# Decode attention with a gated MLP on one core: the up projection in 12 small pieces instead of 3 bursts

## The chip, the core and the metric

The kernel runs on one core of a Trainium2 chip. The core has five engines with instruction queues of their own: TensorE (PE in the profile; PEld is its weight load), VectorE (DVE), ScalarE (ACT), GpSimd (POOL) and SyncE (SP), which here only issues transfers. Each queue runs in order; engines wait for one another through semaphores. 16 DMA engines move data between the device memory and the on-chip buffer. The metric is the device time of one execution in microseconds (us); lower is better.

## The reference, cut to what matters

One decode step for a batch of B = 8, D = 576, 32 heads of 128, 4096 cached keys and values per head, and beside it an MLP with a hidden width of 4608; a gate mixes the two.

```python
q = (x @ wq).reshape(B, 1, 32, 128).transpose(0, 2, 1, 3)
scores = einsum("bhqd,bhkd->bhqk", q, k_cache) * 128 ** -0.5
o = einsum("bhqk,bhkd->bhqd", softmax(scores), v_cache)
a = o.transpose(0, 2, 1, 3).reshape(B, 1, 4096) @ wo
...
h = gelu(einsum("bsd,df->bsf", layernorm(x), w1) + b1)
b = einsum("bsf,fd->bsd", h, w2) + b2
...
g = sigmoid((x * gate_w).sum(-1, keepdims=True))
out = g * a + (1 - g) * b
```

The K and V caches are 256 MiB each in bf16 and are read once. The weights come to about 20 MB.

## The kernel before, in words

**Groups.** The (batch, head) pairs are worked in 32 groups of 8 heads of one batch (`NG` = 32, loop at L593). A group has 8 MiB of K and 8 MiB of V: the 128 partitions are 8 heads x 16 stretches of the sequence, each with 256 positions. K comes in two halves of 128 positions (4 MiB each) into two buffers `KB0` and `KB1`; V comes whole into one buffer, `VB`.

**Scores.** A half has four chunks of 32 positions, so a group has eight, c = 0 to 7. For a chunk DVE multiplies K by q into `p1`, which has two halves used in turn (`mult`, L413); TensorE sums pieces of the 128 products with eight matmuls against a resident identity (`p_sum`, L424 for the first, L169 for the seven others, which keep the stationary operand); DVE reduces the result into `s_sb` (`reduce`, L431). `scores` (L435) writes the order out by hand: mult 0, mult 1, then for every c: reduce c, mult c + 2. After each mult, with its eight matmuls, it calls `between(c)`, which places other work at that point of the queues. `mult(c + 2)` waits for the matmuls of chunk c, and the matmuls of a chunk wait for the reduce two chunks back.

**Softmax, P·V and after.** `softmax` (L447) makes the maximum, the exponentials (ACT, L457), the probabilities `P` (L460) and their sum on DVE. On TensorE follow `total` (L481) and 64 matmuls of P against `VB` (`pv`, L474), then ACT's eviction (L486) and `gather` (L491). `norm` of group n - 1 runs on DVE behind mult 1 of group n.

**The queue of transfers.** All large loads go out on SP in program order: x, wq, K and V of group 0, w1 (two parts, L393, waiting for the q projection, since wq, w1, w2 and wo use one buffer, `RB`), and then in every group n the two K halves of n + 1 and V of n + 1. A half of K waits until `mult` 3 or 7 has read the buffer (`k_done`); V waits until `pv(n)` has read `VB` (`v_done`). An issue that waits on SP holds up what is behind it.

**The MLP around the change.** `up_proj(j0, j1)` (L504) runs 6 matmuls with 8 moving columns each for every one of the 36 tiles of the hidden width (`NJ`): 4 with a 128-wide and 2 with a 64-wide stationary operand, into the PSUM bank `up_ps`; 216 in all. Before the change it runs in 3 calls of 12 tiles (72 matmuls), behind chunk 6 of group 1 and chunks 2 and 6 of group 2. `act_h` (L515) is the gelu: five DVE operations and a sigmoid on ACT, behind chunk 7 of group 2. `load_w2` and `load_b2` follow at the end of group 2. `down_proj` (L547, `quarters` at L533) runs 36 x 4 matmuls in two calls of 18 tiles in group 4, `b_out` (L552) behind them; `load_wo` follows at the end of group 4. `a_proj` uses wo from group 30 on. TensorE's instructions are written out for groups 0 to 4 and from 29 on; groups 5 to 28 are one loop of 24 turns (`emit_loop`, L97; `L0`, `L1`).

Of the kernel before, what the change touches and what calls it, by code (L numbers as in the profile page):

```python
# [20 lines left out]
NJ = F // 128  # L21
# [3 lines left out]
NHG = H // HB  # L25
NG = NHG * B
NTT = SK // RH
NKH = 2
NTK = NTT // NKH
CT = 32  # L30
NCK = NTK // CT
NC = NKH * NCK
# [9 lines left out]
class Stream:  # L42
# [9 lines left out]
    def op(self, engine, fn, waits=(), dma=None):  # L52

        rec = [fn, [w for w in waits if w is not None], None, dma]
        self.ops[engine].append(rec)
        if dma is not None:
            return ("dma", *dma)
        return ("op", engine, rec)
# [75 lines left out]
def bass_gated_mix__mha_block_cached__mixer_channel_mlp__decode_kernel(  # L134
# [20 lines left out]
    def pstride(t):  # L155
        return t[tuple([slice(None)] * len(t.shape))].ap[0][0]
# [122 lines left out]
    def load_k(u):  # L279
        n, s = divmod(u, NKH)  # L280
        nK[s] += 1
        src = kv_src(A_k_cache, n)[:, s * NTK:(s + 1) * NTK, :]
        k_land[u] = op("sync", lambda e: e.dma_start(KB[s][:, :, :], src), [k_done.get(u - NKH)], dma=(sK[s], 16 * nK[s]))
# [7 lines left out]
    def load_v_part(n, buf, at, t0, t1, waits):  # L291

        src = kv_src(A_v_cache, n)[:, t0:t1, :]
        dst = buf[:, at:at + t1 - t0, :]
        t = load("sync", dst, src, f"sVp{n}_{t0}", waits)
        v_land.setdefault(n, []).append((t, buf, at - t0, t0, t1))
# [102 lines left out]
    def q_of(b):  # L399
        for i in range(2):  # L400
            t = op("tensor", lambda e, i=i: e.matmul(
                qb_ps[64 * i:64 * i + 64, :], lhsT=Sel[:, b, :],
                rhs=bass.AP(tensor=Q4, offset=i * DH, ap=[[pstride(Q4), 128], [2 * DH, NHG], [1, DH]]),
                start=True, stop=True), [*a_Q, c_Sel, a_qb.get(b - 1)] if i == 0 else ())
        a_qb[b] = op("scalar", lambda e: e.activation(out=q_bc[:, b, :], in_=qb_ps[:, :], func=ACT.Copy), [t])
# [29 lines left out]
    def scores(n, between):  # L435

        mult(n, 0)
        between(0)
        mult(n, 1)
        between(1)  # L440
        for c in range(NC):
            reduce(n, c)
            if c + 2 < NC:
                mult(n, c + 2)
                between(c + 2)
# [34 lines left out]
    def total(n):  # L480
        p_z[n] = op("tensor", lambda e: e.matmul(  # L481
            oz_ps[:, HB:2 * HB], lhsT=ones[:, :], rhs=rs[:, :], start=True, stop=True),
            [v_rs[n], v_norm.get(n - 1), c_ones])
# [11 lines left out]
    def norm(n):  # L495
        hg, b = divmod(n, B)
        t = op("vector", lambda e: e.reciprocal(out=rz[:, :], in_=oz_ps[:, HB:2 * HB]), [p_oz[n]])  # L497
        v_norm[n] = op("vector", lambda e: e.tensor_tensor(
            out=OT_sb[:, hg * HB:(hg + 1) * HB, b], in0=oz_ps[:, 0:HB], in1=rz[:, :], op=ALU.mult), [t])
# [4 lines left out]
    def up_proj(j0, j1):  # L504
        for jt in range(j0, j1):
            for kt in range(NKF + 2):
                o, n, at = up_ps[:, jt * B:(jt + 1) * B], 128, kt * F + jt
                if kt >= NKF:
                    o, n, at = up_ps[64 * (kt - NKF):64 * (kt - NKF) + 64, jt * B:(jt + 1) * B], 64, NKF * F + jt
                w = bass.AP(tensor=RB, offset=at, ap=[[pstride(RB), 128], [NJ, n]])  # L510
                st["p_up"] = op("tensor", lambda e, w=w, o=o, kt=kt: e.matmul(  # L511
                    o, lhsT=w, rhs=yT_sb[:, kt, :], start=(kt == 0), stop=(kt >= NKF)),
                    [*ld_w1, v_yT] if jt == kt == 0 else ())

    def act_h():  # L515
        hb, t2 = (up[:, i, :] for i in range(2))
        b1b = bass.AP(tensor=b1_sb, offset=0, ap=[[pstride(b1_sb), 128], [1, NJ], [0, B]])
        t = op("vector", lambda e: e.tensor_tensor(
            out=hb.rearrange("p (f b) -> p f b", b=B), in0=up_ps[:, 0:NJ * B].rearrange("p (f b) -> p f b", b=B),
            in1=b1b, op=ALU.add), [st["p_up"], ld_b1])  # L520
        st["v_hb"] = t
        t = op("vector", lambda e: e.tensor_tensor(out=t2, in0=hb, in1=hb, op=ALU.mult), [t])
        t = op("vector", lambda e: e.tensor_scalar(out=t2, in0=t2, scalar1=0.044715, scalar2=1.0, op0=ALU.mult,
                                                   op1=ALU.add), [t])
        t = op("vector", lambda e: e.tensor_tensor(out=t2, in0=t2, in1=hb, op=ALU.mult), [t])
        t = op("scalar", lambda e: e.activation(out=t2, in_=t2, func=ACT.Sigmoid, scale=gelu_c), [t])
        st["v_h"] = op("vector", lambda e: e.tensor_tensor(
            out=hT_sb[:].rearrange("p f b -> p (f b)"), in0=hb, in1=t2, op=ALU.mult), [t])
# [4 lines left out]
    def quarters(lhsT, w, first, stop, waits):  # L533

        for i in range(4):
            last = op("tensor", lambda e, i=i: e.matmul(
                y_ps[32 * i:32 * i + B, 0:QN], lhsT=lhsT, rhs=w[:, i * QN:(i + 1) * QN], start=first, stop=stop),
                waits if i == 0 else ())
        return last
# [7 lines left out]
    def down_proj(j0, j1):  # L547
        for jt in range(j0, j1):
            st["p_down"] = quarters(hT_sb[:, jt, :], w2_sb[:, jt, :], jt == 0, jt == NJ - 1,
                                    [st["ld_w2"], st["v_h"], c_yps] if jt == 0 else ())  # L550

    def b_out():  # L552
        st["v_bx"] = op("vector", lambda e: e.tensor_tensor(
            out=bmg_sb[0:QP, :], in0=y_ps[0:QP, 0:QN], in1=b2_4[0:QP, :], op=ALU.add), [st["p_down"], *st["ld_b2"]])
        st["v_bmg"] = op("vector", lambda e: e.tensor_scalar(
            out=bmg_sb[0:QP, :], in0=bmg_sb[0:QP, :], scalar1=g4[0:QP, 1:2], scalar2=None, op0=ALU.mult),
            [st["v_bx"], v_g4])
# [4 lines left out]
    def a_proj(hg):  # L562
        for h in range(hg * HB, (hg + 1) * HB):
            st["p_a"] = quarters(OT_sb[:, h, :], wo_sb[:, h, :], h == 0, h == H - 1,
                                 [v_norm[hg * B + B - 1], st["ld_wo"], st["v_bx"]] if h == hg * HB else ())
# [17 lines left out]
            [p_oz[n], v_rz[n]])  # L583


    UP0, UPN = 3, 3
    DN = 4
    AP = 30
    L0, L1 = 5, 29
    done_a = [0]  # L590
    last = NG - 1
    q_of(0)
    for n in range(NG):  # L593
        if L0 <= n <= L1:
            S.marks.append(len(S.ops["tensor"]))

        def between(c, n=n):
            u = n * NKH + c // NCK
            c4 = c % NCK
            if c == 1 and 1 <= n < last:  # L600
                norm(n - 1)
            if n == last and c == NCK:
                load_v_part(n, KB[0], 0, 0, NTK, [k_done[NKH * n]])
                t0 = NTK
                for nt in V_LAST:
                    load_v_part(n, VB, t0 - NTK, t0, t0 + nt, [p_pv[n - 1]])
                    t0 += nt
            if c4 == 2:
                if UP0 <= u < UP0 + UPN:
                    up_proj((u - UP0) * NJ // UPN, (u - UP0 + 1) * NJ // UPN)  # L610
                if n == DN:
                    down_proj((c // NCK) * NJ // 2, (c // NCK + 1) * NJ // 2)
                if n >= AP and done_a[0] < NHG - 1:
                    a_proj(done_a[0])
                    done_a[0] += 1
            if c4 == 3:
                if u == UP0 + UPN - 1:
                    act_h()
                if n == DN and c > NCK:
                    b_out()  # L620
            if n == 0 and c + 1 < B:
                q_of(c + 1)

        scores(n, between)
        softmax(n)
        if n < last:
            total(n)
        if n < last - 1:
            load_k(NKH * (n + 1))
            load_k(NKH * (n + 1) + 1)  # L630
            pv(n, (0,))
            evict(n)
            gather(n)
            if n + 1 < last - 1:
                load_v(n + 1)
        if n == last - 2:
            load_v_part(last - 1, VB, 0, 0, NTK, [v_done[n]])
        if n == last - 1:
            load_k(NKH * last)
            load_k(NKH * last + 1)  # L640
            load_v_part(n, VB, NTK, NTK, NTT, [v_done[n - 1]])
            pv(n, (0,))
        if n * NKH <= UP0 + UPN - 1 <= n * NKH + 1:
            load_w2()
            load_b2()
        if n == DN:
            load_wo()
# [60 lines left out]
```

## Time and profile before

| | us |
|---|---|
| median of 3 runs | 1315.97 (1313.71 to 1316.01) |
| the profiled execution | 1315.18 |
| its span, first to last instruction | 1313.4 |
| TensorE busy in it | 815.9 (62%) |
| VectorE busy | 856.8 (65%) |
| ScalarE busy | 47.9 (4%) |
| read from memory | 556.96 MB, 424 GB/s over the span |

How to read the profile: times are from the start of the span. The page divides the span into 40 slices of 32.8 us and gives a busy share of each in tenths, the clock that TensorE was granted (PEclk; 1.0 is full speed), and the DMA engines' busy share. Groups of instructions are named by line, engine, operation and tiles (out<-in), with count, busy time, mean length of one in ns, and the idle time of the engine ahead of them with what ended it (`<-`). "The chain" is the work that ended last, followed back step by step to what released it. Rows of the timeline give start, length, engine, line, operation and tile names; equal neighbours are merged (x72 is 72 instructions), and a matmul's end is modelled, so neighbouring rows can overlap a little.

### The profile page before, as it was taken

To read this page: it belongs to the slowest core of one execution; us is meant where nothing else is said; L and a number is where in the kernel's file an instruction comes from. 1 tells how busy PE (TensorE), PEld (TensorE's weight loads), DVE (VectorE), ACT (ScalarE), POOL (GpSimd) and SP (SyncE) were. 2 spreads that over 40 slices of the span, in tenths; PEclk is the share of its full clock that TensorE was granted. 3 is DMA by queue.
4 is the path that set the end of the run, shared out by engine and by line. 5 is a ranking of instruction groups with operands and counts; after the bars stand their busy time and mean duration, and the time that the engine had idled before them with its cause. 6 is when DMAs were issued, how large, how long until landed. Compare 5 with 4: busy or idle time off the path is not lost.

```text
span 1313.4 us, 10207 instructions
## 1 busy us (share of the span) xinstructions
PE 815.9 (62%) x5156; PEld 170.7 (13%) x3364; DVE 856.8 (65%) x1094; ACT 47.9 (4%) x81; POOL 1.6 (0%) x12
## 2 busy tenths in 40 slices
PE   3647765655666666666565666565666666666666
PEld 0103311110111100111110111110111110011113
DVE  4565574556666677666677666668665667766685
ACT  1100000000000000000000000000000000000000
POOL 0000000000000000000000000000000000000000
PEclk8867797887887888787888878888977888878788
DMA  9999989999999999999999999999999999999997
GB/s 400 426 437 442 392 357 442 432 408 446 423 441 418 432 431 432 442 431 439 420 431 434 443 425 439 420 433 433 433 444 423 439 422 431 433 444 428 425 403 292
DMA packets 20904, 557.28 MB, mean 424 GB/s; under 512 B 2048, under 2 KB 6160, under 8 KB 7056
## 3 DMA queue, kind: packets, MB, share of 16 engines
q1 hardware_dynamic: 20624, 556.95, 98.7%
q8 instruction: 13, 0.21, 0.1%
q14 instruction: 11, 0.09, 0.0%
q10 hardware_dynamic: 256, 0.03, 0.0%
HBM read 556.96 MB, written 0.01 MB: 424 GB/s over the span
## 4 chain that ended last, share of the span: by engine, by line
DMA 64%; DVE 21%; PE 13%; issue 0%; SPq 0%; ACT 0%
DMA KB<-in_A_k_cache_dram 63%; DVE p L413 17%; PE psb L169 8%; DVE s_sb L431 4%; DMA VB<-in_A_v_cache_dram 2%; PE psb L424 2%; PE psb L511 1%; PE psb L474 1%; SPq L250 0%; DVE P L460 0%; PE psb L491 0%; PE psb L481 0%; ACT E L457 0%; DVE mA L448 0%; ACT O_sb L486 0%
## 5 line engine op out<-in xcount | busy, mean ns | idle before, releaser
L413 DVE TENSOR_TENSOR p<-KB,q_bc 128x4096 bf16<-128x4096 bf16 x256 | 581.9, 2283 | 310.3 <-DMA KB<-in_A_k_cache_dram 310.3
L169 PE MATMUL psb<-p,ident 128*128 128x512 bf16 x1792 | 487.8, 418 | 0.0
L424 PE MATMUL psb<-p,ident 128*128 128x512 bf16 x256 | 111.6, 436 | 299.2 <-DVE p L413 298.8
L431 DVE TENSOR_REDUCE s_sb<-psb 128x32 f32<-128x512 f32 x256 | 175.6, 686 | 91.8 <-PE psb L169 91.6
L474 PE MATMUL psb<-VB,P 128*32 128x512 bf16 x1984 | 176.5, 534 | 0.3 <-DMA VB<-in_A_v_cache_dram 0.2
L424 PEld LDWEIGHTS psb<-p,ident 128*128 128x128 bf16 x256 | 26.4, 103 | 738.9 <-DVE p L413 651.2
L481 PE MATMUL psb<-rs,ones 128*128 128x8 f32 x64 | 18.8, 367 | 155.5 <-DVE rs L464 154.9
L474 PEld LDWEIGHTS psb<-VB,P 128*32 128x32 bf16 x1984 | 64.5, 129 | 98.7 <-issue 83.1
L460 DVE TENSOR_SCALAR P<-E,own 128x256 bf16<-128x256 bf16 x248 | 51.5, 283 | 17.9 <-ACT E L457 17.9
L457 ACT ACTIVATE E<-s_sb,mD 128x256 bf16<-128x256 f32 x32 | 16.2, 507 | 919.5 <-DVE mD L456 919.5
L491 PE MATMUL psb<-selO,O_sb 128*128 128x8 f32 x248 | 33.6, 262 | 21.2 <-ACT O_sb L486 21.2
L481 PEld LDWEIGHTS psb<-rs,ones 128*128 128x128 f32 x64 | 15.8, 307 | 214.9 <-DVE rs L464 214.3
L491 PEld LDWEIGHTS psb<-selO,O_sb 128*128 128x128 f32 x248 | 30.8, 195 | 36.1 <-ACT O_sb L486 36.1
L486 ACT ACTIVATE O_sb<-psb 128x512 f32<-128x512 f32 x31 | 18.5, 596 | 259.0 <-PE psb L474 259.0
L511 PE MATMUL psb<-yT_sb,RB 128*128 128x8 bf16 (+1 forms) x216 | 19.6, 229 | 0.0
L511 PEld LDWEIGHTS psb<-yT_sb,RB 128*128 128x128 bf16 (+1 forms) x216 | 18.6, 165 | 5.7 <-issue 4.3
L448 DVE TENSOR_REDUCE mA<-s_sb 128x1 f32<-128x256 f32 x32 | 13.4, 420 | 1.1
L497 DVE RECIPROCAL rz<-psb 128x8 f32<-128x8 f32 x31 | 6.3, 202 | 11.3 <-PE psb L491 11.3
L463 DVE TENSOR_REDUCE es<-E 128x1 f32<-128x256 bf16 x32 | 13.2, 413 | 0.0
L387 PE MATMUL psb<-RB,p 128*8 128x512 bf16 x40 | 5.6, 626 | 5.3 <-DMA RB<-in_A_wq_dram 5.3
L464 DVE TENSOR_SCALAR rs<-own,es 128x8 f32<-128x8 f32 x32 | 7.4, 231 | 1.1
L456 DVE STREAM_TRANSPOSE mD<-mC 128x32 f32<-128x32 f32 x32 | 6.8, 212 | 1.1
(69 smaller groups left out, 86.2 us busy)
## 6 DMA issues: line engine op xcount, KB each, us to landing
KB<-in_A_k_cache_dram SPq DMA_DIRECT2D x64, 4096.0 KB, 26.9
VB<-in_A_v_cache_dram SPq DMA_DIRECT2D x2, 4096.0 KB, 24.0
RB<-in_B_w_dram SPq DMA_DIRECT2D x1, 5184.0 KB, 33.8
RB<-in_B_w_dram SPq DMA_DIRECT2D x1, 4608.0 KB, 45.6
RB<-in_A_wo_dram SPq DMA_DIRECT2D x1, 4608.0 KB, 45.3
RB<-in_A_wq_dram SPq DMA_DIRECT2D x1, 4096.0 KB, 12.4
KB<-in_A_v_cache_dram SPq DMA_DIRECT2D x1, 4096.0 KB, 17.8
VB<-in_A_v_cache_dram SPq DMA_DIRECT2D x2, 1024.0 KB, 21.0
```

The source lines that it names most:

```text
L169: return e.add_instruction(mybir.InstMatmult(name=nc.get_next_instruction_name(), engine=mybir.EngineType.PE, ins=[e.lower_ap(rhs), e.lowe ...
L413: v_mult[n, c] = op("vector", lambda e: e.tensor_tensor(out=p1[:, par, :, :], in0=KB[u % NKH][:, t0:t0 + CT, :], in1=qb, op=ALU.mult), [k_ ...
L424: fn = lambda e, r=r: e.matmul(tr_ps[par][:, :], lhsT=ident[:, :], rhs=r, start=True, stop=False)
L431: v_red[n, c] = op("vector", lambda e: e.tensor_reduce(out=s_sb[:, c * CT:(c + 1) * CT], in_=tr_ps[par][:, :].rearrange("p (t c) -> p t c" ...
L448: t = op("vector", lambda e: e.tensor_reduce(out=mA[:, 0:1], in_=s_sb[:, :], axis=AX.X, op=ALU.max), [v_red[n, NC - 1], c_mA])
L457: a_exp[n] = op("scalar", lambda e: e.activation(out=E[:, :], in_=s_sb[:, :], func=ACT.Exp, bias=mD[:, 0:1], scale=1.0), [v_nm[n], v_P.get ...
L460: v_P[n] = op("vector", lambda e, h=h: e.tensor_scalar(out=(P if n < NG - 1 else P_last)[:, :, h, :], in0=E[:, :].rearrange("p (q t) -> p ...
L474: p_pv[n] = op("tensor", lambda e, o=o, tq=tq, at=at, buf=buf: e.matmul(o, lhsT=P[:, tq, :, :].rearrange("p h t -> p (h t)"), rhs=buf[:, a ...
L481: p_z[n] = op("tensor", lambda e: e.matmul(oz_ps[:, HB:2 * HB], lhsT=ones[:, :], rhs=rs[:, :], start=True, stop=True), [v_rs[n], v_norm.ge ...
L486: a_ev[n] = op("scalar", lambda e: e.activation(out=O_sb[:].rearrange("p t d -> p (t d)"), in_=o_ps[0][:, :], func=ACT.Copy), [p_pv[n], p_ ...
L491: p_oz[n] = op("tensor", lambda e, tt=tt: e.matmul(oz_ps[:, 0:HB], lhsT=O_sb[:, tt, :], rhs=selO[:, tt, :], start=(tt == 0), stop=(tt == T ...
L511: st["p_up"] = op("tensor", lambda e, w=w, o=o, kt=kt: e.matmul(o, lhsT=w, rhs=yT_sb[:, kt, :], start=(kt == 0), stop=(kt >= NKF)), [*ld_w ...
```

## The change

The up projection is called 12 times with 3 tiles (18 matmuls) each, behind chunks 1, 3, 5 and 7 of groups 1, 2 and 3. The gelu moves behind chunk 3 of group 4; `load_w2` and `load_b2` to the end of group 3; the down projection is called 4 times with 9 tiles each, behind chunks 0, 2, 4 and 6 of group 5, with `b_out` behind chunk 7; `load_wo` moves to the end of group 5. `DN` becomes 5, and TensorE's loop covers groups 6 to 29 (`L0` = 6, `L1` = 30). The calls of `a_proj` keep their places. What is computed is the same.

```diff
-    UP0, UPN = 3, 3
-    DN = 4
+    UP, NUP = 1, 3
+    DN = UP + NUP + 1
     AP = 30
-    L0, L1 = 5, 29
+    L0, L1 = DN + 1, 30
...
         def between(c, n=n):
-            u = n * NKH + c // NCK
-            c4 = c % NCK
...
-            if c4 == 2:
-                if UP0 <= u < UP0 + UPN:
-                    up_proj((u - UP0) * NJ // UPN, (u - UP0 + 1) * NJ // UPN)
-                if n == DN:
-                    down_proj((c // NCK) * NJ // 2, (c // NCK + 1) * NJ // 2)
-                if n >= AP and done_a[0] < NHG - 1:
-                    a_proj(done_a[0])
-                    done_a[0] += 1
-            if c4 == 3:
-                if u == UP0 + UPN - 1:
-                    act_h()
-                if n == DN and c > NCK:
-                    b_out()
+            if c % 2 == 1 and UP <= n < UP + NUP:
+                i = (n - UP) * NC // 2 + c // 2
+                up_proj(i * NJ * 2 // (NUP * NC), (i + 1) * NJ * 2 // (NUP * NC))
+            if n == UP + NUP and c == 3:
+                act_h()
+            if n == DN and c % 2 == 0:
+                down_proj(c * NJ // NC, (c + 2) * NJ // NC)
+            if n == DN and c == NC - 1:
+                b_out()
+            if n >= AP and c % NCK == 2 and done_a[0] < NHG - 1:
+                a_proj(done_a[0])
+                done_a[0] += 1
...
-        if n * NKH <= UP0 + UPN - 1 <= n * NKH + 1:
+        if n == UP + NUP - 1:
             load_w2()
             load_b2()
```

## The prediction

> **What bounds the kernel now.** I read the page first: the row of the DMA engines' busy share, the bandwidth under it, and the share of each engine in the chain of work that ended last.
>
> ```profile
> DMA  9999989999999999999999999999999999999997
> GB/s 400 426 437 442 392 357 442 432 408 446 423 441 418 432 431 432 442 431 439 420 431 434 443 425 439 420 433 433 433 444 423 439 422 431 433 444 428 425 403 292
> ...
> DMA 64%; DVE 21%; PE 13%; issue 0%; SPq 0%; ACT 0%
> ```
>
> The transfers are the bound: every slice but one before the last is 90% busy or more. The exception is the sixth (164 to 197 us, 8 tenths, 357 GB/s), just behind the groups that hold the up projection. So I cut the span there with the windows view (length; PE, PEld, DVE, ACT and POOL busy; then granted clock, DMA share, GB/s).
>
> ```profile
> 74.00:162.00 88.00, 64.88 (x419) 23.94 (x307) 55.41 (x72) 4.62 (x6) 0.00 (x0) 0.77 1.01 433
> 162.00:170.00 8.00, 7.29 (x73) 3.32 (x73) 4.23 (x2) 0.60 (x1) 0.00 (x0) 0.65 0.20 72
> 170.00:1274.00 1104.00, 683.34 (x4039) 123.78 (x2468) 740.55 (x926) 30.32 (x55) 0.00 (x0) 0.84 1.00 431
> ```
>
> The queue is full from 74 to 162 us and from 170 to 1274 us. Between them it stands: at a share of 0.20, 8 x 0.80 = 6.4 us are idle; by bytes, 8 x (1 - 72/431) = 6.7 us. I take 6.5. Everything behind this hole runs at the pace of the queue, so a microsecond closed here is a microsecond off the end. The chain, piece by piece (start, length, what), shows what filled the time ahead of it.
>
> ```profile
> 36.33 41.08 DMA KB<-in_A_k_cache_dram
> ...
> 99.60 6.40 PE psb L511 x72
> ...
> 177.86 34.70 DMA KB<-in_A_k_cache_dram
> ```
>
> From 36.33 + 41.08 = 77.4 us to 177.9 us the chain holds no transfer: groups 1, 2 and half of 3 are bound by compute, with bursts of 72 up-projection matmuls (L511) on it, of which this is the first of three. SP's own timeline shows which issue was late.
>
> ```profile
> 121.07 0.33 SPq L288 DMA_DIRECT2D VB<-in_A_v_cache_dram  x1
> 130.29 17.88 SPq L283 DMA_DIRECT2D KB<-in_A_k_cache_dram  x2
> 168.65 0.33 SPq L288 DMA_DIRECT2D VB<-in_A_v_cache_dram  x1
> ```
>
> The V load of group 3 went out at 168.65, because it waits for group 2's P·V matmuls (L474), which read VB. At 431 GB/s a 4 MiB half of K takes 9.7 us and the 8 MiB of V 19.5 us. The queue ran dry at about 162.4. Counted back from there in the order of issue: the K halves of group 3 began at 142.9, V of group 2 at 123.5, the K halves of group 2 at 104.0. So **the due times** are 123.5 us for V of group 2 (met by 2.4 us) and 162.4 for V of group 3 (missed by 6.3).
>
> **What a burst costs.** TensorE's timeline around the first one, then what DVE did behind it, then one window:
>
> ```profile
> 94.90 0.39 PE L424 MATMUL psb<-p,ident 128*128 128x512 bf16 x1 [0.90 <-DVE p L413]
> 95.13 1.67 PE L169 MATMUL psb<-p,ident 128*128 128x512 bf16 x7
> 97.70 0.39 PE L424 MATMUL psb<-p,ident 128*128 128x512 bf16 x1 [0.90 <-DVE p L413]
> 97.92 1.67 PE L169 MATMUL psb<-p,ident 128*128 128x512 bf16 x7
> 99.44 6.56 PE L511 MATMUL psb<-yT_sb,RB 128*128 128x8 bf16 x72
> 105.93 0.61 PE L424 MATMUL psb<-p,ident 128*128 128x512 bf16 x1
> 106.33 3.19 PE L169 MATMUL psb<-p,ident 128*128 128x512 bf16 x7
> 114.52 0.59 PE L481 MATMUL psb<-rs,ones 128*128 128x8 f32 x2 [5.00 <-DVE rs L464]
> 115.05 5.98 PE L474 MATMUL psb<-VB,P 128*32 128x512 bf16 x64
> 121.73 1.06 PE L491 MATMUL psb<-selO,O_sb 128*128 128x8 f32 x8 [0.71 <-ACT O_sb L486]
> ```
>
> ```profile
> 109.56 0.69 DVE L431 TENSOR_REDUCE s_sb<-psb 128x32 f32<-128x512 f32 x1 [8.52 <-PE psb L169]
> ```
>
> ```profile
> 130.00:140.00 10.00, 10.00 (x76) 5.56 (x65) 3.73 (x5) 0.00 (x0) 0.00 (x0) 0.67 1.01 439
> ```
>
> DVE paces a chunk at 97.70 - 94.90 = 2.80 us. The eight score matmuls hold TensorE for 99.44 - 97.70 = 1.74 us at full clock; then it waits for the next product, 0.90 us by the profile's idle. The burst lasts 105.93 - 99.44 = 6.49 us, 90 ns a matmul, and DVE waits 8.52 us for what is behind it: a chunk at half clock too, 109.52 - 105.93 = 3.59 us to its end where the one before took 1.89, so 1.74 + 1.70 = 3.44 us from start to start. The window says that TensorE was busy 10 of 10 us at a mean granted clock of 0.67: the 8-column matmuls do not keep the clock up.
>
> **The change, part by part.** (1) Twelve pieces of 18 matmuls follow chunks 1, 3, 5 and 7 of groups 1 to 3. A piece lasts 6.49 / 4 = 1.62 us. A pair of chunks leaves TensorE 2 x 0.90 = 1.80 us idle, so at full clock a piece lies under DVE's work; without that cover it costs 1.62, or 6.5 a group. The exception is the first pair of a group: behind two half-clock chunks TensorE is late by 2 x (3.44 - 2.80) = 1.3 us, so there I charge 1.3 a group, between nothing and one piece. All 216 matmuls remain; the identity is loaded at each chunk (L424) already, so no load is added.
>
> What is a group worth without bursts? Group 7 of this trace, which DVE also begins by waiting for K; the DVE rows that open groups 2 and 7, then SP's issues in group 7:
>
> ```profile
> 116.21 4.50 DVE L413 TENSOR_TENSOR p<-KB,q_bc 128x4096 bf16<-128x4096 bf16 x2 [1.74 <-DMA KB<-in_A_k_cache_dram]
> ...
> 342.50 4.49 DVE L413 TENSOR_TENSOR p<-KB,q_bc 128x4096 bf16<-128x4096 bf16 x2 [9.01 <-DMA KB<-in_A_k_cache_dram]
> ```
>
> ```profile
> 353.98 11.53 SPq L283 DMA_DIRECT2D KB<-in_A_k_cache_dram  x2
> 377.78 0.33 SPq L288 DMA_DIRECT2D VB<-in_A_v_cache_dram  x1
> ```
>
> From the landing of K to the next V issue it takes 377.78 - 342.50 = 35.3 us; with 1.3 for the first pair, 36.6. Group 1: K landed at 77.4, so V of group 2 goes out near 114.0, against 121.07 now and 123.5 due. Group 2: K lands at 116.2 as now, since that transfer's place in the queue does not move, so V of group 3 goes out at 152.8, **9.6 us before** its due time instead of 6.3 after. Its P·V finds V of group 2 there: that ends at 142.9, and landing took K 116.2 - (104.0 + 9.7) = 2.5 us more. Group 3: K lands at 142.9 + 9.7 + 2.5 = 155.1, V of group 4 goes out at 191.7; due is 162.4 + 19.5 + 19.5 = 201.4. The hole closes and none opens behind it.
>
> (2) Gelu moves to chunk 3 of group 4, the down projection to four pieces in group 5 (two in group 4 now); the loads of w2 and wo go one group later, and with w2 the four small b2 loads on ACT, which has 0% of the chain. DVE's rows around gelu, a down piece on TensorE, the loads of w1, and their issue:
>
> ```profile
> 153.41 0.46 DVE L518 TENSOR_TENSOR Q<-psb,b_sb 128x288 f32<-128x288 f32 x1 [5.60 <-PE psb L511]
> ...
> 156.09 0.68 DVE L431 TENSOR_REDUCE s_sb<-psb 128x32 f32<-128x512 f32 x1
> ```
>
> ```profile
> 223.35 1.30 PE L536 MATMUL psb<-RB,hT_sb 128*8 128x144 bf16 x72
> ```
>
> ```profile
> RB<-in_B_w_dram SPq DMA_DIRECT2D x1, 4608.0 KB, 45.6
> ...
> RB<-in_B_w_dram SPq DMA_DIRECT2D x1, 576.0 KB, 46.6
> ```
>
> ```profile
> 20.65 0.93 SPq L250 DMA_DIRECT2D RB<-in_B_w_dram  x2
> ```
>
> Gelu holds DVE 156.09 - 153.41 = 2.7 us, without the 5.6 us wait, since the last up piece is then half a group old. Group 4 starts with K at 162.4 + 19.5 + 9.7 + 2.5 = 194.1 and issues V at 194.1 + 35.3 + 2.7 = 232.1. V of group 4 ends at 220.9, w2 (5.3 MB, 12.3 us) and two K halves follow it to 252.7, so the 2.7 is covered seven times over; without cover it is 2.7. A down piece is half of 1.30, under one chunk's 0.90. On SP w2 stands behind the V load, which already waits for group 3's P·V and so for all up pieces: no new wait there. wo stands behind group 5's in the same way. K of group 5 comes behind w2 as K of group 4 does now; the queue is full meanwhile. Pieces from chunk 1 of group 1 on need w1: issued by 21.6, landed 46.6 us later, at 68.2, before group 1 begins. (3) TensorE's instruction loop covers groups 6 to 29 instead of 5 to 28, again 24 turns. Moving its entry and exit costs between nothing and the 9.0 us for which DVE waits for K in a group such as 7; I take nothing, since a stall shorter than that wait is hidden.
>
> **Sum.** The profiled execution took 1315.18 us (its span and 1.8 around it); the median of the runs shown is 1315.97, 0.8 above it. Take away 6.5, add nothing: 1308.7, on the median 1309.5. I say **1308.9**.
>
> [...] The 0.67 above is how the clock behaves here. [...]
>
> **The rivals.** *The clock stays at half in groups 1 to 3: slower.* The pieces put work that loses the clock behind every pair, and TensorE becomes the bound. A pair takes 2 x 3.44 + 1.62 = 8.50 us, four 34.0. Group 1: 77.4, 2.2 for the first product (half of 4.5), 34.0 less the last piece, 5.5 from the last sum to P·V (109.56 to 115.05) and 6.0 for it, 123.5: just due. From one V issue to the next: 32.4, 5.5, 6.0 and 1.7 for eviction and gather (121.03 to 122.79) are 45.6, against 38.9 of queue; 6.7 are lost in group 2 and again in group 3. 13.4 - 6.5 = 6.9 slower: 1322.1. [...] It decides only where nearly every pair is slow: one costs 8.50 - 5.60 = 2.9, and it takes more than three in group 2 to use up the margin of 9.6. [...]
>
> *Part of the hole stays.* The clock is lost in most pairs of groups 1 and 2 and held in group 3. Half the hole, 3.2 us, remains: 1312.0. Against: the same margin.
>
> *The end does not move.* The time saved comes back as a wait near the end, where DVE's progress and not the queue issues the last pieces of V. Time 1315.2. For: the last slice's 7 tenths. Against: 1104 us at a share of 1.00, so the last groups start as much earlier as the queue does.
>
> **How the numbers follow.** Forecast 77%, part of the hole 10%, unmoved 6%, slower 7%. Below 1308.9 lie a hole of 6.7 and the spread of the runs shown (1313.71 to 1316.01): 1306.4. Upward the range takes in the partial case and 0.6 us more, 1312.6, and leaves 13% beyond. 0.2% is 2.6 us, about what can be told from no change. Forecast and partial case are faster by more, less one in a hundred at the edge: 0.86; same 0.07; slower 0.07.
>
> **What would show it.** Right: between 74 and 1270 us no window of 8 us with a DMA share under 0.9; the V issues near 114, 153 and 192; L511 in pieces of about 1.6 us, with a clock near 1.0 from chunk 2 to 7 of groups 1 to 3; the last transfers as now but some 6.5 us earlier. Wrong: a clock of 0.5 across these groups with TensorE gapless, a hole ahead of V of group 3 or 4, or a tail that has grown.

## The result, and the profile after

| | before | after |
|---|---|---|
| median of the runs, us | 1315.39 (1313.71 to 1316.01, 4 runs) | 1308.68 (1308.35 to 1308.83, 4 runs) |
| ratio, 95% interval | | 0.9950 (0.9935 to 0.9965) |
| the profiled execution / its span, us | 1315.18 / 1313.4 | 1308.57 / 1306.8 |

The forecast was 1308.9, and 1308.7 against the profiled execution. The interval lies below 1. The same rows of the page as before, now of the changed kernel:

```profile
DMA  9999999999999999999999999999999999999996
GB/s 402 417 447 424 440 422 440 432 434 408 442 430 435 423 432 431 437 430 435 430 427 433 432 442 431 430 427 433 434 437 438 428 428 433 432 434 440 421 406 279
...
DMA 69%; DVE 20%; PE 10%; SPq 0%; issue 0%; ACT 0%
```

The sixth slice went from 8 tenths and 357 GB/s to 9 and 422, and the transfers' part of the chain from 64% to 69%. The windows view of the changed kernel (PE, PEld, DVE, ACT and POOL busy; then clock, DMA share, GB/s):

```profile
74.00:162.00 88.00, 64.79 (x431) 22.00 (x310) 58.66 (x72) 2.21 (x4) 0.00 (x0) 0.81 1.00 432
162.00:170.00 8.00, 8.00 (x58) 3.41 (x38) 7.80 (x6) 0.00 (x0) 0.00 (x0) 0.97 1.16 504
170.00:1267.00 1097.00, 677.38 (x4041) 125.39 (x2499) 733.45 (x923) 33.35 (x58) 0.00 (x0) 0.84 1.00 431
```

The hole at 162 to 170 us is gone: the share there is 1.16, at 504 GB/s. In short windows this view's share can pass 1: in the run with doubled pieces below it reads 0.15 to 2.35 in the single microseconds from 85 to 102 us, and 1.03 over all of them. The long stretch runs at 431 GB/s as before. SP issues the stores of the output at 1304.47 us instead of 1311.08, 6.6 us earlier. SP's timeline of the changed kernel gives the issues:

```profile
113.19 0.33 SPq L288 DMA_DIRECT2D VB<-in_A_v_cache_dram  x1
127.68 11.52 SPq L283 DMA_DIRECT2D KB<-in_A_k_cache_dram  x2
152.93 0.33 SPq L288 DMA_DIRECT2D VB<-in_A_v_cache_dram  x1
166.68 11.82 SPq L283 DMA_DIRECT2D KB<-in_A_k_cache_dram  x2
191.36 0.33 SPq L288 DMA_DIRECT2D VB<-in_A_v_cache_dram  x1
```

V of group 3 went out at 152.93 instead of 168.65, 9.5 us ahead of its due time. The chain, piece by piece, of the changed kernel:

```profile
36.74 40.68 DMA KB<-in_A_k_cache_dram
...
89.14 27.06 DMA KB<-in_A_k_cache_dram
...
127.68 27.28 DMA KB<-in_A_k_cache_dram
```

The 100 us without a transfer are gone from it: already in group 1 it goes back to the queue at 89.14, and no up-projection matmul stands on it. TensorE's timeline of the changed kernel in group 1 and one window there:

```profile
89.17 0.39 PE L424 MATMUL psb<-p,ident 128*128 128x512 bf16 x1 [0.36 <-DVE p L413]
89.40 1.67 PE L169 MATMUL psb<-p,ident 128*128 128x512 bf16 x7
90.91 1.65 PE L511 MATMUL psb<-yT_sb,RB 128*128 128x8 bf16 x18
92.49 0.39 PE L424 MATMUL psb<-p,ident 128*128 128x512 bf16 x1
92.72 1.67 PE L169 MATMUL psb<-p,ident 128*128 128x512 bf16 x7
94.77 0.39 PE L424 MATMUL psb<-p,ident 128*128 128x512 bf16 x1 [0.38 <-DVE p L413]
```

```profile
85.00:102.00 17.00, 15.88 (x105) 5.54 (x61) 15.92 (x12) 0.00 (x0) 0.00 (x0) 1.00 1.03 442
```

From 89.17 to 94.77 is 5.60 us, DVE's own pace for two chunks, with the piece inside (90.91 to 92.49, 1.58 us); TensorE still waits for DVE once a pair, and the clock is 1.00.

### The profile page after: what moved, and what is told of

Same layout as the page of the kernel before. It is cut to its first block, busy times and chain, and to the rows that moved or that the text cites. A ratio compares the mean times of both kernels' runs of the same rounds, so it can differ in the third digit from the quotient of the medians.

```text
span 1306.8 us, 10206 instructions
## 1 busy us (share of the span) xinstructions
PE 812.2 (62%) x5156; PEld 170.7 (13%) x3364; DVE 856.6 (66%) x1094; ACT 47.9 (4%) x81; POOL 1.6 (0%) x12
## 4 chain that ended last, share of the span: by engine, by line
DMA 69%; DVE 20%; PE 10%; SPq 0%; issue 0%; ACT 0%
DMA KB<-in_A_k_cache_dram 67%; DVE p L413 16%; PE psb L169 8%; DVE s_sb L431 3%; DMA VB<-in_A_v_cache_dram 2%; PE psb L424 2%; SPq L250 0%; PE psb L474 0%; DVE P L460 0%; PE psb L536 0%; PE psb L481 0%; PE psb L401 0%; ACT E L457 0%; DVE mA L448 0%; PE psb L572 0%
## 5 line engine op out<-in xcount | busy, mean ns | idle before, releaser
L481 PE MATMUL psb<-rs,ones 128*128 128x8 f32 x64 | 18.4, 360 | 150.9 <-DVE rs L464 150.4
L481 PEld LDWEIGHTS psb<-rs,ones 128*128 128x128 f32 x64 | 15.4, 299 | 201.9 <-DVE rs L464 201.2
L450 DVE STREAM_TRANSPOSE mB<-mA 128x32 f32<-128x32 f32 x32 | 6.8, 212 | 1.1
```

Source lines behind the costliest of these rows:

```text
L481: p_z[n] = op("tensor", lambda e: e.matmul(oz_ps[:, HB:2 * HB], lhsT=ones[:, :], rhs=rs[:, :], start=True, stop=True), [v_rs[n], v_norm.ge ...
```

## The experiments

Three theories were set against one another. **Cover**: the hole closes because the up matmuls lie where TensorE waits for DVE, so P·V ends in time for the next V issue. **Move**: it closes because gelu and the load of w2 come a group later. **Burst**: a burst of 72 opens it wherever it stands, by its length and the clock that it loses. In the runs of the first four experiments the kernel before had a median of 1314.43 us (1313.30 to 1315.93, 19 runs), in those of the last three 1315.15 (1313.31 to 1316.02, 13 runs).

### The spreading alone

```diff
-                if UP0 <= u < UP0 + UPN:
-                    up_proj((u - UP0) * NJ // UPN, (u - UP0 + 1) * NJ // UPN)
+            if c % 2 == 1 and 1 <= n <= 2:
+                i = (n - 1) * 4 + c // 2
+                up_proj(i * NJ // 8, (i + 1) * NJ // 8)
```

> The kernel before with one thing changed: the up projection goes in 8 pieces (24 or 30 matmuls) behind the odd chunks of groups 1 and 2; gelu, w2, down projection, wo and the loop stay where they were. Cover theory (the hole closes because the up matmuls lie under DVE's work): a piece of 2.2 to 2.7 us stands against 1.80 us of idle time in a pair, 0.4 to 0.9 us a pair; with 1.3 for the first pair and 2.7 for gelu, V of group 3 goes out 36.6 + 2.5 + 2.7 = 41.8 us after K landed at 116.2, at 158, before its due time of 162.4: 1308.7 us, up to 1310.5 if some pairs lose the clock. Move theory (the hole closes because gelu and the loads of w2 come a group later): the hole stays, 1315.

Measured: 1308.25 us (1308.10 to 1308.59), ratio 0.9953 (0.9936 to 0.9970). SP's timeline:

```profile
114.56 0.33 SPq L288 DMA_DIRECT2D VB<-in_A_v_cache_dram  x1
128.01 13.55 SPq L283 DMA_DIRECT2D KB<-in_A_k_cache_dram  x2
160.10 0.33 SPq L288 DMA_DIRECT2D VB<-in_A_v_cache_dram  x1
```

V of group 3 went out at 160.1, 2.3 us ahead of the due time, and the whole gain is there with gelu, w2 and the rest in their old places. The move theory falls. It went out two microseconds later than expected. DVE's timeline of this run and one window (columns as above) show where:

```profile
146.38 0.46 DVE L518 TENSOR_TENSOR Q<-psb,b_sb 128x288 f32<-128x288 f32 x1 [5.18 <-PE psb L511]
```

```profile
134.00:138.00 4.00, 4.00 (x12) 0.29 (x2) 2.82 (x3) 0.00 (x0) 0.00 (x0) 0.59 0.78 332
```

Gelu stands behind the last product of group 2, and the last piece behind that chunk's sums: DVE waited 5.18 us for it, where only gelu's own 2.7 had been counted. And the clock was lost for a while in group 2, 0.59 from 134 to 138 us, behind a piece of 30 matmuls.

### The moves alone

```diff
-            if c % 2 == 1 and UP <= n < UP + NUP:
-                i = (n - UP) * NC // 2 + c // 2
-                up_proj(i * NJ * 2 // (NUP * NC), (i + 1) * NJ * 2 // (NUP * NC))
+            if (n, c) in ((1, 6), (2, 2), (2, 6)):
+                i = ((1, 6), (2, 2), (2, 6)).index((n, c))
+                up_proj(i * NJ // 3, (i + 1) * NJ // 3)
```

> The changed kernel with the up projection back in three bursts of 72 matmuls behind chunk 6 of group 1 and chunks 2 and 6 of group 2; gelu, w2, down projection, wo and the loop at their new places. Cover theory: the bursts make V of group 3 late as before. Gelu's 2.7 us gave nothing to the path, because DVE waited another 0.16 us for the half-clocked last chunk after it. The hole stays at 6 to 7 us: 1315. Move theory: 1309.

Measured: 1315.03 us (1313.48 to 1315.76, 10 runs), ratio 1.0002 (0.9992 to 1.0012). SP's timeline, and the DVE row behind the third burst:

```profile
120.77 0.33 SPq L288 DMA_DIRECT2D VB<-in_A_v_cache_dram  x1
129.98 17.89 SPq L283 DMA_DIRECT2D KB<-in_A_k_cache_dram  x2
168.26 0.33 SPq L288 DMA_DIRECT2D VB<-in_A_v_cache_dram  x1
```

```profile
156.63 0.69 DVE L431 TENSOR_REDUCE s_sb<-psb 128x32 f32<-128x512 f32 x1 [8.52 <-PE psb L169]
```

The V issue is as late as before (168.26 against 168.65). With gelu taken out of group 2, DVE simply waits 8.52 us for the burst and the chunk behind it, as long as behind the first burst of the kernel before, where the granted clock was 0.75 in the burst (99.5 to 106 us) and 0.50 in that chunk (106 to 109.6).

### Three bursts where TensorE waits for the softmax

```diff
-            if c % 2 == 1 and UP <= n < UP + NUP:
-                i = (n - UP) * NC // 2 + c // 2
-                up_proj(i * NJ * 2 // (NUP * NC), (i + 1) * NJ * 2 // (NUP * NC))
+            if c == 7 and UP <= n < UP + NUP:
+                i = n - UP
+                up_proj(i * NJ // NUP, (i + 1) * NJ // NUP)
```

> The changed kernel with the up projection in three bursts of 72 matmuls, one behind chunk 7 of groups 1, 2 and 3, all else as changed. Cover theory: behind the last chunk TensorE waits some 5.1 us for the softmax, so a burst of 6.5 us is covered but for 1.4; V loads go out near 114.6, 154.3 and 192.8 us, all before their due times: 1308.7. Burst theory (a burst of 72 costs the hole wherever it stands, by its length and the clock lost): 1313 to 1315.

Measured: 1308.56 us (1308.36 to 1308.75), ratio 0.9955 (0.9938 to 0.9971). TensorE's timeline in group 1, the end of the softmax on DVE there, then SP's timeline:

```profile
101.58 6.53 PE L511 MATMUL psb<-yT_sb,RB 128*128 128x8 bf16 x72
108.04 0.60 PE L481 MATMUL psb<-rs,ones 128*128 128x8 f32 x2
```

```profile
106.45 0.23 DVE L464 TENSOR_SCALAR rs<-own,es 128x8 f32<-128x8 f32 x1
```

```profile
152.82 0.33 SPq L288 DMA_DIRECT2D VB<-in_A_v_cache_dram  x1
166.41 11.53 SPq L283 DMA_DIRECT2D KB<-in_A_k_cache_dram  x2
192.61 0.33 SPq L288 DMA_DIRECT2D VB<-in_A_v_cache_dram  x1
```

The burst is covered but for 108.04 - 106.68 = 1.4 us, as expected: the first matmul behind it (L481) needs the softmax, which ends at 106.45 + 0.23 = 106.68 us. V of group 4 goes out at 192.6, 1.2 us later than with small pieces (191.36), but well ahead of its due time of 201.4, so nothing of it reaches the end. The V issues are at 152.8 and 192.6, where 154.3 and 192.8 were expected. The burst theory falls: a burst of 72 does not open the hole wherever it stands. This run has one burst in each of three groups, where the kernel before has two in group 2; the next experiment keeps that number and changes only the place.

### Three bursts one chunk earlier

```diff
-            if c == 7 and UP <= n < UP + NUP:
+            if c == 6 and UP <= n < UP + NUP:
```

(against the experiment before this one)

> As burst_c7, but the three bursts stand behind chunk 6 of groups 1, 2 and 3, where one chunk is still to come. Cover theory: a burst exposes 6.5 us less 0.9, and the last chunk at half clock 1.7 more, 7.3 a group. V of group 2 near 120.5 (due 123.5). Group 2 then starts late by some 2 us: V of group 3 near 162.5, due 162.4, hole 0 to 1.5. Group 3: V near 204, due 201.4 and the hole before, 2 to 3. Together 2 to 4.5: 1311 to 1313. If only the number of bursts in a group counted, 1308.7.

Measured: 1311.06 us (1309.45 to 1312.61, 10 runs), ratio 0.9974 (0.9965 to 0.9984). The profiled execution is the shortest of the ten, at 1309.45. Its SP timeline, then one window of this run and the same window of the changed kernel:

```profile
160.60 0.33 SPq L288 DMA_DIRECT2D VB<-in_A_v_cache_dram  x1
169.81 11.53 SPq L283 DMA_DIRECT2D KB<-in_A_k_cache_dram  x2
201.41 0.33 SPq L288 DMA_DIRECT2D VB<-in_A_v_cache_dram  x1
```

```profile
170.00:240.00 70.00, 48.97 (x324) 14.56 (x232) 44.22 (x63) 5.22 (x7) 0.00 (x0) 0.83 0.98 418
170.00:240.00 70.00, 42.91 (x282) 11.53 (x198) 41.41 (x61) 5.22 (x7) 0.00 (x0) 0.84 0.98 422
```

V of group 4 goes out at its due time (201.4) to a tenth, and from 170 to 240 us the queue moves a little less than in the changed kernel, 418 GB/s against 422, which is 0.7 us of 70. So with a single chunk left behind each burst the margin is used up, and this execution loses 0.9 us (1309.45 - 1308.57; 0.6 by the spans, 1307.4 and 1306.8). The issues expected at 162.5 and 204 came earlier, at 160.6 and 201.4, and this execution lies below the expected 1311 to 1313; the median lies inside. That the longer ones lose more at the same place fits the theory, but none of them was profiled.

Two comparisons are worth making. Against the bursts behind chunk 7, with as many bursts in each group, the median is 2.5 us longer: the place counts. Against the moves alone, whose same three bursts stand behind chunk 6 of group 1 and twice in group 2, it is 4.0 us shorter (1311.06 against 1315.03): how many bursts lie ahead of one V issue counts as well. By the number of bursts in a group alone 1308.7 was expected.

### Pieces of twice and three times the length

Every up tile is computed twice, or three times, over itself:

```diff
-            for kt in range(NKF + 2):
+            for kt in [k for k in range(NKF + 2)] * 2:
```

> The changed kernel with every up tile computed twice (the second time over the first), so each of the 12 pieces has 36 matmuls and the rest is as changed. Cover theory at full clock: a piece of 3.24 us against 1.80 of idle time, 1.44 exposed a pair, 5.8 a group and 1.4 in the first pair; V of group 3 near 160, due 162.4: no hole, 1308.7. Clock rival: score matmuls fill only 3.48 of 6.72 us of a pair, 52%; if that loses the clock, a pair costs up to 3.4 us more and holes of 2 to 5 us open ahead of V of groups 3 and 4: 1311 to 1318.

> As pieces_x2 with every tile computed three times, 54 matmuls a piece. Cover theory: a piece of 4.86 us, a pair of at least 8.34; from one V issue to the next 4 x 8.34 - 4.9 + 5.1 + 5.7 + 1.7 = 41 us against 38.9 of queue, so holes open even at full clock: 1312 to 1314; with the clock at half, a pair of 11.7 and holes of 8 or more in three groups, 1325 to 1335. If the end did not hang on these V issues, 1308.7.

Measured: twice, 1308.51 us (1308.46 to 1308.62), ratio 0.9949 (0.9933 to 0.9966); three times, 1330.91 (1329.24 to 1331.38), ratio 1.0115 (1.0098 to 1.0132). Of the run with doubled pieces, a window of group 1 and one of group 3; on TensorE the beginning of one pair and of the next, and P·V of group 2; and two SP rows:

```profile
85.00:102.00 17.00, 17.00 (x144) 9.90 (x113) 14.87 (x11) 0.00 (x0) 0.00 (x0) 1.00 1.03 446
165.00:170.00 5.00, 5.00 (x24) 1.10 (x13) 1.44 (x3) 0.00 (x0) 0.00 (x0) 0.66 1.11 475
```

```profile
95.08 0.39 PE L424 MATMUL psb<-p,ident 128*128 128x512 bf16 x1
...
101.77 0.39 PE L424 MATMUL psb<-p,ident 128*128 128x512 bf16 x1
...
148.44 5.33 PE L474 MATMUL psb<-VB,P 128*32 128x512 bf16 x64
```

```profile
116.29 0.33 SPq L288 DMA_DIRECT2D VB<-in_A_v_cache_dram  x1
...
153.82 0.33 SPq L288 DMA_DIRECT2D VB<-in_A_v_cache_dram  x1
```

Doubled, TensorE does not wait in these two windows, and the clock is full in group 1, but not behind the first piece of group 3 (0.66 from 165 to 170 us). The pieces are no longer covered: a pair with its piece takes 101.77 - 95.08 = 6.69 us, 1.09 more than DVE's 5.60, and V of group 2 goes out at 116.29, 3.1 us later than with single pieces. That costs no time, since it is due at 123.5. V of group 3 goes out only 0.9 us later (153.82), and the 160 expected was too pessimistic. One thing it had counted wrongly is the number of exposed pieces: the fourth lies under the softmax, for which TensorE still waits 1.86 us behind it in group 1. Another lies outside the pieces: P·V of group 2 took 5.33 us here and 6.55 with single pieces, which takes 1.2 us back. The windows of the run with three times the length:

```profile
122.00:129.00 7.00, 6.27 (x70) 2.88 (x70) 4.36 (x2) 0.60 (x1) 0.00 (x0) 0.71 0.37 143
129.00:166.00 37.00, 37.00 (x246) 16.59 (x190) 19.02 (x17) 0.00 (x0) 0.00 (x0) 0.72 0.99 415
166.00:177.00 11.00, 10.05 (x116) 6.54 (x114) 7.65 (x17) 1.11 (x2) 0.00 (x0) 0.84 0.48 180
177.00:214.00 37.00, 37.00 (x247) 16.67 (x190) 19.21 (x17) 0.00 (x0) 0.00 (x0) 0.72 0.95 401
214.00:225.00 11.00, 10.04 (x114) 6.47 (x114) 7.46 (x17) 1.17 (x3) 0.00 (x0) 0.84 0.48 180
225.00:1290.00 1065.00, 656.77 (x3899) 118.89 (x2385) 715.90 (x898) 32.29 (x56) 0.00 (x0) 0.84 1.00 431
```

Here the clock drops to a mean of 0.72, TensorE is busy without a gap for 37 us in a group, and three holes open. Against 431 GB/s the five stretches lose 4.7 + 1.4 + 6.4 + 2.6 + 6.4 = 21.5 us; the span is 1329.4 - 1306.8 = 22.6 longer. This is the prediction's slower rival made real, though by three times the work, and it shows that holes in these groups go to the end nearly microsecond for microsecond.

### The loop alone

```diff
-    L0, L1 = 5, 29
+    L0, L1 = 6, 30
```

> The kernel before with only TensorE's loop moved, to groups 6 to 29. All theories: the entry and the exit cost nothing that is seen, 1315; a stall at the exit would show as a later last transfer.

Measured, on the kernel before: 1315.35 us (1313.93 to 1316.08, 10 runs), ratio 1.0001 (0.9992 to 1.0011). The loop's place costs nothing that can be seen.

## Why the prediction was right

- **The hole, 6.5 us.** The profiled executions differ by 1315.18 - 1308.57 = 6.6 us, their spans by as much. Shown by the windows, and by the runs in which the hole returns (the moves alone, 1315.03) or multiplies (three times the length).
- **A piece is covered.** Forecast 1.62 us under 1.80 of idle time; measured 1.58, with two chunks still at 5.60 us. That the cover decides is shown from both sides: the same bursts of 72 add nothing to the time behind chunk 7 and some 2.5 us in all behind chunk 6 (1311.06 against 1308.56).
- **The charge for the first pair.** Forecast 36.6 us from K's landing to the V issue. Measured 113.19 - 77.45 = 35.7, 152.93 - 116.23 = 36.7 and 191.36 - 154.99 = 36.4, with K's landings from DVE's first products of the three groups. The sum came out, its term did not. TensorE's rows behind the softmax, for group 7 of the kernel before and group 2 of the changed one:

```profile
372.11 0.39 PE L481 MATMUL psb<-rs,ones 128*128 128x8 f32 x2 [5.00 <-DVE rs L464]
372.43 5.29 PE L474 MATMUL psb<-VB,P 128*32 128x512 bf16 x64
```

```profile
145.80 0.59 PE L481 MATMUL psb<-rs,ones 128*128 128x8 f32 x2 [3.51 <-DVE rs L464]
146.32 6.55 PE L474 MATMUL psb<-VB,P 128*32 128x512 bf16 x64
```

From K's landing to L481 it takes 372.11 - 342.50 = 29.6 us in group 7, and 29.8, 29.6 and 30.1 in groups 1 to 3 of the changed kernel, so the first pair cost 0 to 0.5 us where 1.3 was charged. In group 2, whose P·V releases V of group 3, the rest is P·V itself: 6.55 us at a mean clock of 0.55 (146.4 to 152.9 us), against 5.29 at 0.68 (372.5 to 377.7 us). The forecast had taken P·V as in group 7; that the one error made up for the other there is luck, and with a margin of 9.6 us neither could have opened the hole.

- **V issues.** Forecast near 114.0, 152.8 and 191.7; measured 113.2, 152.9, 191.4. The second is so close by the luck just named.
- **Gelu, w2, wo, the loop.** Taken at nothing; the moves alone give 1315.03 and the loop alone 1315.35, neither to be told from before. In the changed kernel gelu held DVE for 207.56 - 204.89 = 2.7 us without a wait, and V of group 5 went out at 232.6 (forecast 232.1).
- **The clock.** The forecast counts a piece at full clock. Score matmuls fill 1.74 of 2.80 us of a chunk before the change and 2 x 1.74 of 5.60 us of a pair with its piece, 62% both times; that this share holds the clock was the author's estimate, and no run shows it. The clock held: 1.00 from 85 to 102 us in group 1, 1.00 from 122 to 145 in group 2, 0.94 from 167 to 185 in group 3. The rival's mechanism exists all the same: with pieces three times as long the clock is lost (a mean of 0.72 from 129 to 166 us) and the time is 22 us above the changed kernel's. Pieces twice as long still cost nothing, by the margin to the due times and not by cover.
- **The end.** The rival by which the gain returns as a wait near the end has nothing for it: the queue runs at 431 GB/s until 1267 us, and what is left then takes 1306.8 - 1267 = 39.8 us, where 1313.4 - 1274 = 39.4 were left before.
- **A sign that was too sharp.** No window of 8 us was to have a DMA share under 0.9. From 306 to 314 us it is 0.83, though from 298 to 322 it is 0.99; the kernel before has such windows in its full stretch too (0.84 from 234 to 242). The hole was 0.20, and nothing like it is left.

## What to carry to other kernels

Where transfers bound a kernel, look for the place at which their queue stands still, find the issue that was late, and count the queue back to the time by which it had to go out; that due time says how much work may lie on the path. Here off-path work cost nothing that can be seen where it lay under a wait of its engine for another one: in slices between paced steps (1308.68 us), or whole in a longer wait but for 1.4 us (1308.56). What stuck out cost nothing either while the issue still met its due time: with doubled pieces V of group 2 went out at 116.29 against 123.5, and the time was 1308.51 us. Splitting is one means to that end and not the end itself, as the three unsplit bursts behind the last chunk show.

## What the runs showed that was not expected

- No share of score matmuls can be named that holds the clock. With doubled pieces they fill 2 x 1.74 of 6.69 us, 52%, and the clock was 1.00 from 85 to 102 us and from 121 to 140, but 0.66 from 165 to 170, behind a doubled piece in the same execution. With pieces of 24 and 30 matmuls it fell to 0.59 from 134 to 138. At three times the length, 2 x 1.74 of at least 8.34 us or 42%, the mean was 0.72 with TensorE busy for 37 of 37 us. TensorE was busy throughout in all of these windows, in those at 1.00 (17 of 17 and 19 of 19 us) as in those at 0.59 to 0.72, so being busy alone did not keep the clock; what decides it stays open.
- Where there is a hole, the time also varies. Every kernel whose queue stood still or nearly so ranged over 2 to 3 us (before 1313.30 to 1316.02; the bursts behind chunk 6 from 1309.45 to 1312.61), and those with a full queue over 0.2 to 0.5 us. That the hole's length changes with the clock from run to run is a guess; no run was made for it.
